# Eight small stores of pieces of x to the output's place in the middle of an attention decode kernel

## The chip, the cores and the metric

The kernel runs on one core of a Trainium2 chip. The metric is the device time of one execution in microseconds (us), lower is better. A time is the median of several runs. A change of the time is called real only beyond 0.2%, 1.37 us here.

## The reference

One decode step of attention with a cache, gated by a GLU block. All tensors are float32; D = 512, 32 heads of 128, 8192 cached positions, F = 1376.

```python
xn = layernorm(x)                                   # x: 1 x 1 x 512
q = (xn @ wq) as 32 heads of 128
p = softmax(q . k_cache * 128 ** -0.5)              # over 8192 positions of each head
s = (p . v_cache) as 1 x 4096 @ wo
g = silu((sigmoid(xn @ w_gate) * (xn @ w_up)) @ w_down)
return x + s * g                                    # 1 x 1 x 512
```

Each of the two caches holds 32 x 8192 x 128 values, 134 MB, and each value is used once.

## The kernel before

**Tiling.** Two heads are treated at a time, so there are NP = 16 pairs. The keys of one pair are 2 x 8192 x 128 values; they lie as 128 partitions of 16384 values (64 KB) in one of two slots, `slots[0]` and `slots[1]`, used in turn. The values of a pair lie the same way in `slots[2]`, of which there is one.

**One pair.** `scores(i)` (line 410) is VectorE's part: it multiplies the keys in place by the query (line 415), sums the products over the 128 elements of each position (line 416), and takes the maximum (line 418). ScalarE makes the exponentials (`powers_of`, line 426). TensorE runs a loop of its own, written down as notes and played at the end (`pair`, line 376, recorded with `Later`; therefore all its instructions stand under line 38): it spreads the maximum, then multiplies the weights with the values and counts `valued` up when it has read the whole of them.

**The order of the transfers.** All large loads are issued by SyncE (SP) on one hardware queue, q1, in the order in which the program is written; what SyncE waits for holds back everything behind it. The queue's transfers are carried by 16 DMA engines. In the loop over pairs (line 440), step i first lets SyncE issue the keys of pair i, once the sums of pair i-2 have freed their slot (line 444, through `load_keys` and `load` at line 168), then the values of pair i-1, once TensorE has read those of pair i-2 (line 446, `load_values`, line 227). So at step i = 8 SyncE issues the keys of pair 8 and the values of pair 7, and the next thing in its program is, at step 9, the wait for the sums of pair 7 and the keys of pair 9.

**The start and the end.** x comes in by ScalarE's queue into `x_row` (line 240): 128 of its values in each of four partitions 32 apart, all the rest of the 128 x 128 tile being zero from a memset (line 239). `x_row` is written nowhere else; it is read by the layer norm at the start and by the last addition (line 541). The GLU block runs at the start too, on the first slots. After the last pair, wo is loaded in eight pieces and multiplied by TensorE and VectorE as they land. SyncE then waits for the last addition and stores the result, four rows of 512 bytes, to the output (line 564), clears the semaphores (line 569), and waits for the store's 16 counts on `s_out` (line 571).

Of the kernel before, what the change touches and what calls it, by code (L numbers as in the profile page):

```python
# [13 lines left out]
P = 128  # L14
# [37 lines left out]
def kernel(  # L52
# [17 lines left out]
    HP = P // 2  # L70
    NB = S // HP
    NP = H // 2
    NG = 4
    GP = P // NG
# [22 lines left out]
    DVE, ACT, SP, POOL = nc.vector, nc.scalar, nc.sync, nc.gpsimd  # L97
# [6 lines left out]
    s_out = nc.alloc_semaphore("s_out")  # L104

    def sb(name, *shape):
        return nc.alloc_sbuf_tensor(name, [P, *shape], F32)[:]
# [11 lines left out]
    x_row, g_row = sb("x_row", GC), sb("g_row", GC)  # L119
# [17 lines left out]
    NK = 8  # L137
# [36 lines left out]
    def wait(eng, *steps):  # L174
        for s in steps:
            if s is not None:
                eng.wait_ge(*s)
# [24 lines left out]
    def rows_of(src, i):  # L202
        rows = src.rearrange("b h s d -> (b h s) d")[2 * i * S:2 * (i + 1) * S, :]
        return rows.rearrange("(p j) d -> p (j d)", p=P)
# [3 lines left out]
    def pieces(*ends):  # L208
        return [slice(a, b) for a, b in zip((0,) + ends, ends + (NB,))]
# [3 lines left out]
    def cols(j):  # L213
        return slice(j.start * Dh, j.stop * Dh)

    def load_keys(i, cut, *after):
        n = (i + 1) % 2
        wait(SP, *after)
        for j in cut:
            ld_k.setdefault(i, []).append((j, load(SP, f"k{n}_{j.start}", slots[n][:, cols(j)], rows_of(k_cache, i)[:, cols(j)])))  # L220

    def load_values(i, cut, *after):

        wait(SP, *after)
        for j in cut:
            sem = s_val[((0,) + V_CUTS).index(j.start)]
            SP.dma_start(slots[2][:, cols(j)], rows_of(v_cache, i)[:, cols(j)]).then_inc(sem, 16)  # L227
# [33 lines left out]
    t = dve(DVE.reduce_sum(st[:, 0:1], x_col, axis=AX.X))  # L261
    wait(PE, t)
    t = pe(PE.matmul(pt[:, 0:1], ones, st[:, 0:1], start=True, stop=True))
    wait(DVE, t)
    t = dve(DVE.tensor_scalar(st[:, 1:2], pt[:, 0:1], 1.0 / D, None, op0=ALU.mult))
    wait(DVE, t)
    t = dve(DVE.tensor_scalar(xc, x_col, st[:, 1:2], None, op0=ALU.subtract))
    wait(DVE, t)
    t = dve(DVE.tensor_mul(sq, xc, xc))
    wait(DVE, t)  # L270
    t = dve(DVE.reduce_sum(st[:, 2:3], sq, axis=AX.X))
    wait(PE, t)
    t = pe(PE.matmul(pm[:, 0:1], ones, st[:, 2:3], start=True, stop=True))
    wait(ACT, t)
    t = act(ACT.activation(st[:, 3:4], pm[:, 0:1], AF.Sqrt, bias=eps_t, scale=1.0 / D))
    wait(DVE, t)
    t = dve(DVE.reciprocal(st[:, 4:5], st[:, 3:4]))
# [8 lines left out]
    def in_place(w, k, cols=slice(None)):  # L286
        y = w[:, 0, cols]
        if k == 0:
            return dve(DVE.tensor_scalar(y, y, xn[:, 0:1], None, op0=ALU.mult))
        return dve(DVE.scalar_tensor_tensor(y, w[:, k, cols], xn[:, k:k + 1], y, op0=ALU.mult, op1=ALU.add))  # L290
# [3 lines left out]
    for k in range(KT - 1):  # L294
        wait(DVE, ld_wq[k // 2] if k % 2 == 0 else None, t if k else None)
        t = in_place(wq_t, k)
# [7 lines left out]
    for t in range(NQ):  # L304
        c = slice(t * QT, (t + 1) * QT)
# [26 lines left out]
    rows = []  # L332
    chunks = [slice(c, min(c + QT, F)) for c in range(0, F, QT)]
    sums = (big[0], po, wide[0]), (big[1], wide[1], wide[2])
    for dst, src, ld in zip(sums, (wg_t, wu_t), (ld_g, ld_u)):
        wait(DVE, ld)
        for k in range(KT):
            t = in_place(src, k)
# [7 lines left out]
    for d, c in zip(sums[0], chunks):  # L346
        t = act(ACT.activation(sg[:, c], d[:, :c.stop - c.start], AF.Sigmoid))
    wait(DVE, t, rows[1])
    for d, c in zip(sums[1], chunks):
        t = dve(DVE.tensor_mul(hg[:, c], sg[:, c], d[:, :c.stop - c.start]))  # L350
# [6 lines left out]
    n = FL // NG  # L357
    for g in range(NG):
        r = slice(g * GP, (g + 1) * GP)
        h = hg[r, NG * FW + g * n:NG * FW + (g + 1) * n].rearrange("p (i c) -> p c i", c=FC)  # L360
        t = dve(DVE.transpose(hid[r, FP:, :].rearrange("p c (i m) -> p c i m", m=NG),
                              h.unsqueeze(3).to_broadcast([GP, FC, n // FC, NG])))
    wait(PE, t, ld_d)
    for c in range(FP + FC):
        g = c % NG * GP
# [40 lines left out]
    def all_max(i):  # L406
        DVE.wait_ge(turned, i + 1)
        DVE.reduce_max(mx[:1, 1:3], pt[0:1, :].rearrange("o (e p) -> o e p", e=2), axis=AX.X).then_inc(reduced, 1)  # L408

    def scores(i):  # L410
        k = slots[(i + 1) % 2].rearrange("p (j d) -> p j d", d=Dh)
        for j, ld in ld_k[i]:
            wait(DVE, ld)
            n = j.stop - j.start
            wait(DVE, dve(DVE.tensor_mul(k[:, j, :], k[:, j, :], qb[:, i:i + 1, :].to_broadcast([P, n, Dh]))))  # L415
            summed[i] = dve(DVE.reduce_sum(sc[i % 2][:, j], k[:, j, :], axis=AX.X))  # L416
        wait(DVE, summed[i])
        DVE.reduce_max(mx[:, 0:1], sc[i % 2], axis=AX.X).then_inc(maxed, 1)

    def heads_out(i):  # L420
        DVE.wait_ge(picked, i + 1)
        o = o_t[:, 2 * WP * i:2 * WP * i + Dh].rearrange("r (e a) -> r a e", a=WP)
        turned_out[i] = dve(DVE.transpose(o, pn.rearrange("e (a r) -> e a r", r=WR)))  # L423


    def powers_of(i):
        ACT.wait_ge(spread_m, i + 1)
        wait(ACT, act(ACT.mul(nb, pm[:, :2], -SCALE)))  # L428
        for e, h in enumerate(HALF):
            ACT.activation(weights[h, :, e * HT:(e + 1) * HT], sc[i % 2][h].rearrange("p (g b) -> p g b", b=HT),  # L430
                           AF.Exp, bias=nb[h, e:e + 1], scale=SCALE, accum_out=rs[h]).then_inc(powers, 1)

    def parts(i):
        ACT.wait_ge(added, i + 1)
        t = act(ACT.copy(den[:GP, 2 * i:2 * i + 2], pm[:GP, 2:]))
        ACT.wait_ge(valued, i + 1)
        ACT.copy(o1, po).then_inc(copied, 1)  # L437
        return t

    for i in range(NP):  # L440
        if i > 0:
            all_max(i - 1)
        if i >= 2:
            load_keys(i, pieces(*K_CUTS.get(i, ())), summed[i - 2])
            if i < NP - 1:
                load_values(i - 1, FULL, (valued, i - 1))
        if i == NP - 1:
            for v, cut in ((i - 1, V_HALVES), (i, V_THREE)):
                load_values(v, cut[:1], (halved, v))
                load_values(v, cut[1:], (valued, v))  # L450
        scores(i)
        if i > 0:
            powers_of(i - 1)
            parts(i - 1)
            heads_out(i - 1)
        if i == 1:
            wait(DVE, c_sig)
            c_gate = dve(DVE.tensor_mul(g_row, g_row, big[1][:, :GC]))
# [48 lines left out]
    for k, r in enumerate(W_DVE):  # L507
        n = k % 2
# [30 lines left out]
    t = dve(DVE.tensor_mul(g_row, g_row, acc))  # L539
    wait(DVE, t)  # L540
    t = dve(DVE.tensor_add(g_row, g_row, x_row))  # L541
# [18 lines left out]
    body.close()  # L560
    nc.switch_bb("leave")

    wait(SP, t)
    SP.dma_start(out.rearrange("a b (g c) -> (a b g) c", g=NG), g_row[0:P:GP, :]).then_inc(s_out, 16)


# [1 line left out]
    assert not unused and used == list(range(used[0], used[0] + len(used)))  # L568
    SP.sem_clear(range(used[0], used[-1] + 1))

    SP.wait_ge(s_out, 16)
    SP.nop().then_inc(s_out, -16)


# [26 lines left out]
```

## Time and profile before

| What | Value |
|---|---|
| Median of 3 runs | 685.09 us (684.86 to 685.15) |
| Profiled execution, its own time | 685.13 us |
| Span of the instructions in it | 683.8 us |
| VectorE (DVE) busy | 613.6 us, 90% of the span |
| TensorE (PE) matmuls busy | 227.5 us, 33% |
| Bytes read from HBM | 293.67 MB, 429 GB/s over the span |
| Packets of the transfers | 7264, of them 824 under 512 B |

In the rows of a profile an engine's name is followed by the line of the kernel, the operation, and the names of the tiles as output<-inputs. A q behind an engine's name (SPq, ACTq) marks its instruction queue, as for an issue of a DMA. In a timeline the two leading numbers are the start and the duration in us; a bracket at the end gives the idle time before the instruction and what ended it. In a list of waits the numbers are us in total, times, and the longest. In a table by stretch each engine has its busy time and its number of instructions; the last three columns are the granted TensorE clock, the share of 16 DMA engines that was busy, and GB/s. A packet counts in a stretch with its whole length where it starts, so a short stretch can show a share over 1.

### The profile page before, as it was taken

Reading aid. Unit: us, or ns where it says so; the run is one execution under the profiler, and the core shown is the slowest. Engines: PE = TensorE matmul, PEld = TensorE weight load, DVE = VectorE, ACT = ScalarE, POOL = GpSimd, SP = SyncE. Lnnn points to the kernel's source line nnn. Section 1 sums busy time; section 2 is a strip of 40 time slices with the busy share of each in tenths; the row PEclk is TensorE's granted clock in tenths of the full one; section 3 lists DMA queues with packets and bytes.
Section 4 is the critical chain, followed back from the end, with each engine's and each line's share of the span. In section 5 each row is a group of like instructions: output and inputs, shape, how many; then the busy total and the mean of one; then the engine's idle time right before and its main releaser. Section 6 shows DMA issues by size and latency. Waiting matters only on the chain. (4 is left out here: it accounts for less than half of the span.)

```text
span 683.8 us, 3412 instructions
## 1 busy us (share of the span) xinstructions
PE 227.5 (33%) x1386; PEld 64.6 (9%) x1386; DVE 613.6 (90%) x151; ACT 44.6 (7%) x142; POOL 2.6 (0%) x11
## 2 busy tenths in 40 slices
PE   0363024050513305060513306060512406050777
PEld 0120001010100101010100101010100101010121
DVE  3869999999999998997989898998989899999926
ACT  2130010000000101000000100000010100000010
POOL 0000000000000000000000000000000000000000
PEclk9986557575665757575665757575665757575699
DMA  9999999999999999999999999999999999999997
GB/s 378 430 442 472 429 429 429 429 429 429 429 429 429 429 429 456 449 445 429 429 429 429 429 429 429 429 429 429 460 456 433 429 414 414 460 418 439 429 411 327
DMA packets 7264, 293.67 MB, mean 429 GB/s; under 512 B 824, under 2 KB 832, under 8 KB 1504
## 3 DMA queue, kind: packets, MB, share of 16 engines
q1 hardware_dynamic: 7256, 293.67, 99.4%
q10 hardware_dynamic: 8, 0.00, 0.0%
HBM read 293.67 MB, written 0.00 MB: 429 GB/s over the span
## 5 line engine op out<-in xcount | busy, mean ns | idle before, releaser
L415 DVE TENSOR_TENSOR slot<-slot,q_all 128x16384 f32<-128x16384 f32 (+3 forms) x18 | 275.7, 15319 | 22.8 <-DMA slot<-in_A_k_cache_dram 22.7
L416 DVE TENSOR_REDUCE sc<-slot 128x128 f32<-128x16384 f32 (+3 forms) x18 | 275.8, 15323 | 0.6
L38 PE MATMUL psum<-slot,zeros 128*8 128x512 f32 x1028 | 153.0, 753 | 249.1 <-PEq L38 249.1
L38 PEld LDWEIGHTS psum<-slot,zeros 128*8 128x8 f32 x1028 | 31.1, 104 | 356.3 <-issue 356.3
L38 PE MATMUL psum<-ident,mx 128*1 128x128 f32 x32 | 8.3, 356 | 115.2 <-PEq L38 115.2
L437 ACT COPY o<-psum 128x512 f32<-128x512 f32 x16 | 9.4, 586 | 398.3 <-PE psum L38 398.3
L38 PE MATMUL psum<-slot,ones 128*128 (+3 forms) x36 | 17.4, 657 | 21.7 <-PEq L38 16.2
L290 DVE SCALAR_TENSOR_TENSOR slot<-slot,xn 128x1376 f32<-128x1376 f32 (+1 forms) x8 | 18.9, 2360 | 3.0 <-DMA slot<-in_A_wq_dram 2.7
L38 PE MATMUL psum<-o,pick 128*2 128x128 f32 x128 | 16.5, 272 | 12.8 <-PEq L38 12.8
L423 DVE STREAM_TRANSPOSE psum<-psum 32x128 f32<-32x128 f32 x16 | 5.0, 310 | 9.5 <-PE psum L38 9.5
L38 PE MATMUL psum<-slot,o_all 128*1 128x128 f32 (+1 forms) x60 | 12.5, 421 | 1.8 <-DMA slot<-in_A_wo_dram 1.7
L38 PEld LDWEIGHTS psum<-ident,mx 128*1 128x1 f32 x32 | 1.8, 80 | 119.4 <-issue 119.4
L428 ACT ACTIVATE nb<-psum 128x2 f32<-128x2 f32 x16 | 2.8, 172 | 157.3 <-PE psum L38 157.3
L430 ACT ACTIVATE zeros<-sc,nb 64x128 f32<-64x128 f32 x32 | 12.8, 399 | 0.9
L38 PEld LDWEIGHTS psum<-o,pick 128*2 128x2 f32 x128 | 9.9, 84 | 29.9 <-issue 27.5
L38 PE MATMUL psum<-zeros,rs 128*32 128x2 f32 x32 | 3.8, 188 | 23.5 <-PEq L38 23.5
L408 DVE TENSOR_REDUCE mx<-psum 1x2 f32<-1x128 f32 x16 | 4.5, 279 | 7.7 <-PE psum L38 7.7
L38 PE MATMUL psum<-mx,ones 1*128 1x2 f32 x32 | 8.5, 333 | 7.4 <-PEq L38 7.4
L38 PE MATMUL psum<-slot,o 128*1 128x512 f32 x26 | 6.3, 1025 | 11.6 <-DMA slot<-in_B_w_down_dram 11.6
L38 PEld LDWEIGHTS psum<-slot,ones 128*128 128x128 f32 (+1 forms) x36 | 6.9, 216 | 32.0 <-issue 24.1
L515 DVE SCALAR_TENSOR_TENSOR q_all<-slot,o_all,q_all 128x512 f32<-128x512 f32 x12 | 8.1, 747 | 2.0 <-DMA slot<-in_A_wo_dram 2.0
L38 PEld LDWEIGHTS psum<-mx,ones 1*128 1x128 f32 x32 | 7.6, 292 | 13.9 <-issue 13.9
(54 smaller groups left out, 62.2 us busy)
## 6 DMA issues: line engine op xcount, KB each, us to landing
slot<-in_A_v_cache_dram SPq DMA_DIRECT2D x3, 4096.0 KB, 23.5
slot<-in_A_wq_dram SPq DMA_DIRECT2D x2, 4096.0 KB, 16.3
slot<-in_A_k_cache_dram SPq DMA_DIRECT2D x2, 4096.0 KB, 37.8
slot<-in_A_k_cache_dram SPq DMA_DIRECT2D x1, 6144.0 KB, 37.9
slot<-in_B_w_gate_dram SPq DMA_DIRECT2D x1, 2752.0 KB, 26.7
slot<-in_B_w_up_dram SPq DMA_DIRECT2D x1, 2752.0 KB, 32.6
slot<-in_B_w_down_dram SPq DMA_DIRECT2D x1, 2560.0 KB, 23.2
slot<-in_A_v_cache_dram SPq DMA_DIRECT2D x1, 2560.0 KB, 9.7
```

Of the source, the lines that this page charges most:

```text
L38: ins = getattr(self.engine, name)(*args, **kwargs)
L290: return dve(DVE.scalar_tensor_tensor(y, w[:, k, cols], xn[:, k:k + 1], y, op0=ALU.mult, op1=ALU.add))
L408: DVE.reduce_max(mx[:1, 1:3], pt[0:1, :].rearrange("o (e p) -> o e p", e=2), axis=AX.X).then_inc(reduced, 1)
L415: wait(DVE, dve(DVE.tensor_mul(k[:, j, :], k[:, j, :], qb[:, i:i + 1, :].to_broadcast([P, n, Dh]))))
L416: summed[i] = dve(DVE.reduce_sum(sc[i % 2][:, j], k[:, j, :], axis=AX.X))
L423: turned_out[i] = dve(DVE.transpose(o, pn.rearrange("e (a r) -> e a r", r=WR)))
L428: wait(ACT, act(ACT.mul(nb, pm[:, :2], -SCALE)))
L430: ACT.activation(weights[h, :, e * HT:(e + 1) * HT], sc[i % 2][h].rearrange("p (g b) -> p g b", b=HT), AF.Exp, bias=nb[h, e:e + 1], scale= ...
L437: ACT.copy(o1, po).then_inc(copied, 1)
L515: ins = DVE.scalar_tensor_tensor(part[n], wo_t[:, r, :], col, part[n], op0=ALU.mult, op1=ALU.add)
```

## The change

At step 8 of the loop, between the issue of the values of pair 7 and that of the keys of pair 9, SyncE issues eight more DMAs. Each reads 64 float32 elements of `x_row` and writes them to one eighth (256 bytes) of the output in HBM. Their shapes, partitions x elements: 4 x 16 from partitions 32 apart (twice), 4 x 16 from neighbouring partitions (twice), 16 x 4 from neighbours, 16 x 4 from partitions 8 apart, 64 x 1, and 1 x 64. Each adds 16 to `s_out` when it is done. Ahead of the result's store SyncE now also waits until `s_out` has reached 128, so that the result is written over what the eight stores left; the last wait and the reset of `s_out` are adapted.

```diff
+    extra = 0
     for i in range(NP):
         if i > 0:
             all_max(i - 1)
...
                 load_values(v, cut[1:], (valued, v))
+        if i == 8:
+            pieces_of = out.rearrange("a b (n c) -> n (a b c)", n=8)
+            for n, src in enumerate((x_row[0:P:GP, :2 * NK], x_row[0:P:GP, :2 * NK], x_row[0:NG, :2 * NK],
+                                     x_row[0:NG, :2 * NK], x_row[0:16, :NG], x_row[0:P:8, :NG], x_row[0:HP, :1],
+                                     x_row[0:1, :HP])):
+                rows = pieces_of[n:n + 1, :].rearrange("o (g c) -> (o g) c", g=src.shape[0])
+                SP.dma_start(rows, src).then_inc(s_out, 16)
+                extra += 16
         scores(i)
...
-    wait(SP, t)
+    wait(SP, t, (s_out, extra))
     SP.dma_start(out.rearrange("a b (g c) -> (a b g) c", g=NG), g_row[0:P:GP, :]).then_inc(s_out, 16)
...
-    SP.wait_ge(s_out, 16)
-    SP.nop().then_inc(s_out, -16)
+    SP.wait_ge(s_out, extra + 16)
+    SP.nop().then_inc(s_out, -extra - 16)
```

## The prediction, made before the result was known

> **What bounds the kernel now.** I read the page first: busy shares, slices, DMA queues, and the chain that ended last.
>
> ```profile
> span 683.8 us, 3412 instructions
> PE 227.5 (33%) x1386; PEld 64.6 (9%) x1386; DVE 613.6 (90%) x151; ACT 44.6 (7%) x142; POOL 2.6 (0%) x11
> ...
> DMA  9999999999999999999999999999999999999997
> ...
> q1 hardware_dynamic: 7256, 293.67, 99.4%
> ...
> DMA 4%; PE 1%; SPq 1%; DVE 0%; issue 0%
> ```
>
> Two things are nearly full: VectorE at 90% and SyncE's one transfer queue (q1) at 99.4% of 16 engines. Which of them sets the pace where the stores go is read from that stage: the timeline of VectorE, and then the stretch between two key multiplies by engine.
>
> ```profile
> 351.48 17.23 DVE L415 TENSOR_TENSOR slot<-slot,q_all 128x16384 f32<-128x16384 f32 x1 [2.83 <-DMA slot<-in_A_k_cache_dram]
> 368.74 17.22 DVE L416 TENSOR_REDUCE sc<-slot 128x128 f32<-128x16384 f32 x1
> 390.08 17.23 DVE L415 TENSOR_TENSOR slot<-slot,q_all 128x16384 f32<-128x16384 f32 x1 [2.75 <-DMA slot<-in_A_k_cache_dram]
> ```
>
> ```profile
> core 0: us, PE busy (x) PEld busy (x) DVE busy (x) ACT busy (x) POOL busy (x), PEclk, DMA share, GB/s
> 351.40:390.00 38.60, 11.07 (x78) 3.23 (x78) 35.24 (x5) 1.89 (x7) 0.00 (x0) 0.63 1.00 435
> 652.00:680.30 28.30, 24.17 (x124) 5.35 (x124) 12.30 (x25) 1.89 (x7) 0.00 (x0) 0.94 0.98 415
> ```
>
> VectorE works 35.24 us of each 38.60 us pair of heads and then stands idle, 2.83 and 2.75 us, for the keys. The transfers have no such idle time: share 1.00 at 435 GB/s, and still 0.98 in the last stage, whose end is the landing of wo. So in the middle the queue is the bound, and the rule for this kernel is simple: **time that the 16 DMA engines lose moves the end by as much; time lost elsewhere costs nothing while the queue has work in it.**
>
> How much work it holds when the stores are issued comes from SyncE's own timeline and its landing times.
>
> ```profile
> 341.52 0.33 SPq L227 DMA_DIRECT2D slot<-in_A_v_cache_dram  x1
> 347.31 0.33 SPq L168 DMA_DIRECT2D slot<-in_A_k_cache_dram  x1
> 379.64 0.33 SPq L227 DMA_DIRECT2D slot<-in_A_v_cache_dram  x1
> ```
>
> ```profile
> slot<-in_A_v_cache_dram SPq DMA_DIRECT2D x2, 29.5
> slot<-in_A_k_cache_dram SPq DMA_DIRECT2D x2, 42.7
> ```
>
> The loop step i=8 issues the keys of pair 8 (before this stretch; they release the multiply at 351.48), then the values of pair 7 at 341.52. Values issued at 341.52 land after about 29.5 us, near 371. The keys of pair 9, issued at 347.31, land after 42.7 us, at 390.0. So a transfer waits behind some 20 us of older ones before it begins.
>
> **The change, part by part.** It removes nothing. It adds eight DMA issues on SyncE between the two upper rows of that timeline, eight small transfers in the ring between the values of pair 7 and the keys of pair 9, and a second semaphore to wait for ahead of the result's store. No other engine's program is touched, and the stores wait for nothing.
>
> *Issue time on SyncE.* The keys of pair 9 stand behind the eight issues, and they wait for the sums of pair 7 anyway:
>
> ```profile
> SPq L168 <- DVE sc L416: 5.5, 1, 5.5
> ```
>
> That is the wait in the stretch from 341.9 to 348 us: SyncE stands there 5.5 us with nothing to do. What one issue costs, from the only small ones in the trace, the result's store of four rows and the load of x by ScalarE's queue, and from the groups of wo loads (shortest/median/longest):
>
> ```profile
> 682.08 0.64 SPq L564 DMA_DIRECT2D out_dram<-g_row  x1
> ...
> 2.38 1.08 ACTq L168 DMA_DIRECT2D x_row<-in_A_x_dram  x1
> ```
>
> ```profile
> L168 SPq DMA_DIRECT2D slot<-in_A_wo_dram x8: 430/444/3821, 648.9 to 652.3; - x8
> ```
>
> Eight at 0.64 us are 5.1 us, which fits into the 5.5 us. Eight at 1.08 us are 8.6 us, and the keys would be issued 3.1 us late. Late issue costs nothing at first: the keys cannot begin before the values are through, near 371 us, and begin about 1.2 us after an issue (the result's store is issued at 682.08 and its packets stand at 683.3, below). So they are in time until about 369.5 us, 22 us after 347.31. Cover for the issue time: the values' own transfer. Cost taken: 0; the price without cover is a rival below. The values of pair 8 come next on SyncE, issued at 379.64, 32 us after the keys, so a delay of some us has gone by then.
>
> *Engine time of the stores.* The trace has one small store to HBM, the result's. Its packets, by the queue's view from 683.0 us and by stretches around it:
>
> ```profile
> DMA packets 8, 0.00 MB, mean 3 GB/s; under 512 B 4, under 2 KB 8, under 8 KB 8
> ```
>
> ```profile
> 682.10:683.30 1.20, 0.00 (x0) 0.00 (x0) 0.00 (x0) 0.00 (x0) 0.00 (x0) 1.00 0.00 0
> 683.30:683.40 0.10, 0.00 (x0) 0.00 (x0) 0.00 (x0) 0.00 (x0) 0.00 (x0) 1.00 0.09 21
> 683.40:683.76 0.36, 0.00 (x0) 0.00 (x0) 0.00 (x0) 0.00 (x0) 0.00 (x0) 1.00 0.00 0
> ```
>
> Four rows give eight packets: four of data and four under 512 B, which I read as one completion for each engine that took part. Their engine time is 0.09 x 16 engines x 0.10 us = 0.144 us, 18 ns for each. Now count the stores, one data packet for each row: 4+4+4+4+16+16+64+1 = 113; completions at one per engine used, 4x4 + 16+16+16 + 1 = 65. Together 178, at 18 ns 3.2 us of engine time. Spread evenly over 16 engines that is 0.20 us. An engine that takes part in every store has 4 + 1 + 1 + 4 + 1 = 11 data packets and 8 completions, 19 x 18 ns = 0.34 us. Lower bound: 0, because the engines do not arrive together. At the seam itself, 369.9 to 372.0 us, the completions of the values and the first packets of the keys are these 32:
>
> ```profile
> DMA  0009999990900000000000000000000000000000
> ...
> DMA packets 32, 1.05 MB, mean 499 GB/s; under 512 B 16, under 2 KB 16, under 8 KB 16
> ```
>
> The slices are 2.1/40 = 0.05 us, and the engines pass the seam over eight of them, 0.4 us. Whoever is early can take small packets without holding up the last. Upper bound, if all 113 and eight completions went through one engine: 121 x 18 ns = 2.2 us. I take 0.2 us, the even spread, nearest to the row with four rows on four engines. A gain is excluded here: nothing is taken out of a queue that never idles.
>
> *The extra wait at the end.* The result's store waited for VectorE alone; now it waits for a second semaphore that has long been reached. One separate wait instruction, by the nearest row, TensorE's:
>
> ```profile
> L38 PEldq EVENT_SEMAPHORE  x7: 51/51/51, 370.8 to 389.3; - x7
> ```
>
> 0.05 us, on the path that ends the run; at most twice that with the step between instructions. I take 0.1 us. Below nothing is excluded.
>
> *Sum.* 0 (issue) + 0.2 (engines) + 0.1 (wait) = +0.3 us. The profiled execution took 685.13 us (683.8 span, 1.3 around it); the median of the runs, 685.09, is 0.04 from it. So **685.4 us**, no change that can be told: 0.2% is 1.37 us, about what a measurement of this kernel can tell from none.
>
> **The rivals.**
>
> *A, the ring waits for each store's receipt* (slower). If a store's completion holds its engine until HBM has confirmed the write, every engine that carries all eight stands eight times. The price of one is at most the stretch after the last packet, 683.40 to the end, 0.36 us: 8 x 0.36 = 2.9 us, 688.3 us. It decides from (1.37 - 0.3)/8 = 0.13 us for each store. With the whole way of the result's store, 682.08 to 683.76, as the price it would be 8 x 1.7 = 13.4 us, 698.8 us. For it: the trace holds no store in front of other work. Against it: at the seam at 370 us completions pass with no gap, inside a stretch of share 1.00; but those go to SBUF. The Trainium skill, "DMA: Bandwidth & Descriptors", section "Anatomy of one DMA — SWDGE (gpsimd) path", says that most of a transfer's fixed 2.0 us is the wait for the target's write receipt, and longest for HBM; eight in a row would by that figure be an estimated 16 us, 701 us, if the ring stood still meanwhile, which no run here shows. Chance 0.09.
>
> *B, every small row pays a round trip.* Rows of 4 to 256 bytes may each be read back and merged before the engine goes on. With 0.36 us as price and 11 data packets on the busiest engine: 4.0 us, 689.4 us. It decides from 1.07/11 = 0.10 us each. Against it: the result's rows, written at 18 ns a packet, but they have 512 bytes. The Trainium skill, same page, section "Specifications", states that below 512 B a DMA engine does a read-modify-write, and its section "Latency and other measured facts" gives an HBM access as 0.2 us on average; 11 of those are an estimated 2.2 us, 687.6 us. The 18 ns row does not speak to it, its data packets being just at that size. Chance 0.05.
>
> *C, the keys are issued too late.* If each store's issue took the longest row, 3.82 us, eight take 30.6 us, from 341.85 to 372.4; the keys follow and begin 1.2 us later at 373.6, while the values are through at 371.0: 2.6 us of empty queue, 688.0 us. It decides from (369.5 - 341.85)/8 = 3.5 us an issue. That longest issue was the eighth wo load, behind seven others and two value pieces, so a full ring seems its reason; here the ring holds the rest of one load, the values and the small stores. Chance 0.02.
>
> *D, one engine takes all the rows.* The 2.2 us above: 687.6 us with the wait. Against it: four rows of the result made four completions. Chance 0.02.
>
> **How the numbers follow.** Forecast (0 to 0.34 us of engine time, 0.05 to 0.1 us of wait, and the spread of the runs, 684.86 to 685.15): 0.79, its own range 684.8 to 685.9. A to D: 0.18, all slower. Left over, something that I do not see and that gains: 0.03. So faster 0.03, same 0.79, slower 0.18. The range reaches up over most of the upper bound of the engine time, 2.0 of its 2.2 us above the median and the wait, for the unknown price of a small write: 684.8 to 687.2 us; A, B and C in full stay outside, 0.16.
>
> **What would show it.** In the changed profile: 178 or so more packets under 512 B in q1, all other sizes unchanged; HBM written 2 KB more; the eight issues on SyncE inside the stretch from 341.85 to about 347; the key multiply that stood at 390.08 at most 0.4 us later against the one at 351.48; share 1.00 there. A or B would show as that multiply coming 1 us or more late with an idle stretch of VectorE longer than 2.8 us, and a DMA share under 0.97 between the two; C as a keys issue after 369 us. The prediction is wrong if the distance of these two multiplies grows by more than 1 us, or if the last stage, from 652 us on, changes its length.

## The result and the profile after

The changed kernel takes **690.29 us** (median of 4 runs, 690.04 to 691.46) against 684.98 us before it on the same chip (684.85 to 685.15): a ratio of **1.0082, 95% interval 1.0069 to 1.0094**. It is slower by 5.3 us, far outside the forecast's range of 684.8 to 687.2 us. The profiled execution took 690.09 us, 4.96 more than that of before; its span is 688.4 us, 4.6 more.

From the page of the changed kernel, the packets and the queue:

```profile
span 688.4 us, 3421 instructions
...
DMA packets 7442, 293.68 MB, mean 427 GB/s; under 512 B 1002, under 2 KB 1010, under 8 KB 1682
...
q1 hardware_dynamic: 7434, 293.67, 99.5%
```

There are 178 more packets under 512 B (1002 - 824), the number that the forecast had counted, and the queue is as full as before. The timeline of VectorE around the seam, and then SyncE's:

```profile
351.64 17.22 DVE L415 TENSOR_TENSOR slot<-slot,q_all 128x16384 f32<-128x16384 f32 x1 [2.84 <-DMA slot<-in_A_k_cache_dram]
395.35 17.23 DVE L415 TENSOR_TENSOR slot<-slot,q_all 128x16384 f32<-128x16384 f32 x1 [7.87 <-DMA slot<-in_A_k_cache_dram]
434.03 17.23 DVE L415 TENSOR_TENSOR slot<-slot,q_all 128x16384 f32<-128x16384 f32 x1 [2.83 <-DMA slot<-in_A_k_cache_dram]
```

```profile
341.81 0.33 SPq L227 DMA_DIRECT2D slot<-in_A_v_cache_dram  x1
342.18 4.13 SPq L458 DMA_DIRECT2D out_dram<-x_row  x8
347.46 0.38 SPq L168 DMA_DIRECT2D slot<-in_A_k_cache_dram  x1
```

The multiply of step 8 starts where it did (351.64, before 351.48), that of step 9 comes 43.71 us later instead of 38.60, and the one after that is back at 38.68. The whole loss, **5.1 us, lies in this one step**: VectorE waits 7.87 us for the keys of pair 9 instead of 2.75. SyncE is not the reason: the eight issues take 4.13 us, and the keys are issued at 347.46 (before 347.31). What happened to the transfers shows in two stretches after the stores, and in the whole step:

```profile
core 0: us, PE busy (x) PEld busy (x) DVE busy (x) ACT busy (x) POOL busy (x), PEclk, DMA share, GB/s
351.60:395.30 43.70, 11.20 (x78) 3.27 (x78) 35.24 (x5) 1.89 (x7) 0.00 (x0) 0.62 1.00 384
372.60:380.40 7.80, 7.26 (x60) 1.54 (x52) 7.80 (x1) 0.47 (x1) 0.00 (x0) 0.87 0.99 252
380.40:390.00 9.60, 2.41 (x14) 1.41 (x14) 6.51 (x4) 1.42 (x7) 0.00 (x0) 0.73 0.99 430
```

The engines count as busy throughout (share 0.99 to 1.00), but from 372.6 to 380.4 us they move 252 GB/s, and afterwards 430 again. The loss doesn't show as idle time; it shows only in the last column. The trace also records every packet with its length, and there the loss can be seen. The 178 packets of the stores themselves are short, 9 to 18 ns each, 1.6 us in all or 0.10 us for each engine. But 27 of the 64 KB packets of keys behind them, begun between 370.3 and 377.5 us, last up to 7.5 us, where every such packet of the kernel before lasts 2.42 us in this stretch. What they last beyond 2.42 us adds up to 4.9 us for each of the 16 engines, nearly the whole loss.

What the end shows: the result's store is issued 0.32 us after the start of the last addition in both kernels (682.08 - 681.76 before; here the two rows are at 686.78 and 686.46), so the second semaphore costs nothing. The last addition is 4.70 us later, and not 5.27 as the multiply of step 9 (395.35 - 390.08), because the last stage ran a little shorter. Over the runs below that stage and the rest differ by up to about 1 us either way; therefore **the distance of the two multiplies is taken as the measure of the loss**, and the time of the runs beside it.

### The profile page after: what moved, and what is told of

Read it like the earlier page. It is cut to its first block, busy times and chain, and to the rows that moved or that the text cites. A ratio compares the mean times of both kernels' runs of the same rounds, so it can differ in the third digit from the quotient of the medians.

```text
span 688.4 us, 3421 instructions
## 1 busy us (share of the span) xinstructions
PE 225.0 (33%) x1386; PEld 64.2 (9%) x1386; DVE 613.7 (89%) x151; ACT 44.6 (6%) x142; POOL 2.6 (0%) x11
## 2 busy tenths in 40 slices
DMA packets 7442, 293.68 MB, mean 427 GB/s; under 512 B 1002, under 2 KB 1010, under 8 KB 1682
## 5 line engine op out<-in xcount | busy, mean ns | idle before, releaser
L38 PE MATMUL psum<-slot,zeros 128*8 128x512 f32 x1028 | 150.1, 743 | 254.2 <-PEq L38 254.2
```

The source lines that it names most:

```text
L38: ins = getattr(self.engine, name)(*args, **kwargs)
```

## The experiments

Each kernel is the changed kernel with other stores in the same place of SyncE's program (run 12: of ScalarE's), and so has a wait for their completions at the end. None computes less of the result. "Loss" is the distance of the key multiplies of steps 8 and 9 less the 38.60 us of before, in the one execution that was profiled. In the four runs that lose 0.1 us or less it is 38.61 to 38.68 us.

**1. The column store alone (e1_col64)**

```diff
-            for n, src in enumerate((x_row[0:P:GP, :2 * NK], ..., x_row[0:HP, :1], x_row[0:1, :HP])):
+            for n, src in enumerate((x_row[0:HP, :1],)):
```

> Only the store of 64 rows of 4 bytes stays, 64 of the change's 113 data packets, one of its eight stores; what it loses is read as the distance of the key multiplies of steps 8 and 9, 38.60 us before and 43.71 with all eight, 5.1 us more. Theory 'each packet': every data packet to HBM holds a shared path for 5.1/113 = 0.045 us, so 64 x 0.045 = 2.9 us, distance 41.5. Theory 'each store': every store's receipt costs 5.1/8 = 0.64 us, distance 39.2. Theory 'once': the turn from reading to writing costs 5.1 us however little is written, distance 43.7.

Measured: 690.72 us, ratio 1.0096 (1.0076 to 1.0115). VectorE's timeline:

```profile
351.81 17.23 DVE L415 TENSOR_TENSOR slot<-slot,q_all 128x16384 f32<-128x16384 f32 x1 [2.84 <-DMA slot<-in_A_k_cache_dram]
396.02 17.22 DVE L415 TENSOR_TENSOR slot<-slot,q_all 128x16384 f32<-128x16384 f32 x1 [8.57 <-DMA slot<-in_A_k_cache_dram]
```

Distance 44.21, loss 5.6 us. This one store, 64 rows of 4 bytes written to 256 contiguous bytes, loses as much as all eight together.

**2. The other seven stores (e2_no_col64)**

```diff
-                                     x_row[0:NG, :2 * NK], x_row[0:16, :NG], x_row[0:P:8, :NG], x_row[0:HP, :1],
-                                     x_row[0:1, :HP])):
+                                     x_row[0:NG, :2 * NK], x_row[0:16, :NG], x_row[0:P:8, :NG], x_row[0:1, :HP])):
```

> The other seven stores, without the 64 rows of 4 bytes: 49 data packets. Each packet: 49 x 0.045 = 2.2 us, distance of the two key multiplies 40.8 us. Each store: 7 x 0.64 = 4.5 us, 43.1. Once: 43.7. A fourth, 'the packets of 4 bytes alone are the matter', has 38.6 here and all 5.1 us in the run with the 64 rows.

Measured: 685.35 us, ratio 1.0008 (0.9998 to 1.0017), which cannot be told from no change.

```profile
352.03 17.23 DVE L415 TENSOR_TENSOR slot<-slot,q_all 128x16384 f32<-128x16384 f32 x1 [3.02 <-DMA slot<-in_A_k_cache_dram]
391.01 17.23 DVE L415 TENSOR_TENSOR slot<-slot,q_all 128x16384 f32<-128x16384 f32 x1 [3.13 <-DMA slot<-in_A_k_cache_dram]
```

Loss 0.38 us. "Each store" (4.5 us) and "once" (5.1 us) fall, and "each packet" alike (2.2 us) as well. Seven of the eight stores cost what the forecast had put for all.

**3. The same eight to SBUF (e4_to_sbuf)**

```diff
-                rows = pieces_of[n:n + 1, :].rearrange("o (g c) -> (o g) c", g=src.shape[0])
-                SP.dma_start(rows, src).then_inc(s_out, 16)
+                SP.dma_start(sink[0:src.shape[0], at:at + src.shape[1]], src).then_inc(s_out, 16)
+                at += src.shape[1]
```

> The same eight reads of x, in the same shapes and in the same place of the queue, but to a spare tile in SBUF instead of the output in HBM, so the small rows and the completions stay and the writes to HBM go. If writing to HBM is the cause (each packet, each store or once alike): distance 38.6 to 38.8 us and a time within 0.1% of before. If small packets, odd shapes or completions cost wherever they go: 43.7 us, and 690 us.

Measured: 685.67 us, ratio 1.0011 (1.0001 to 1.0021).

```profile
351.59 17.23 DVE L416 TENSOR_TENSOR slot<-slot,q_all 128x16384 f32<-128x16384 f32 x1 [2.83 <-DMA slot<-in_A_k_cache_dram]
390.73 17.23 DVE L416 TENSOR_TENSOR slot<-slot,q_all 128x16384 f32<-128x16384 f32 x1 [3.30 <-DMA slot<-in_A_k_cache_dram]
```

Loss 0.54 us, a little above the 0.2 us expected: small packets to SBUF are nearly free, the column's 64 among them. (The row of 64 elements went as 16 pieces here, so q1 had 30 packets more than in the changed kernel, 7464 against 7434.) So neither the reads of x nor the number of small packets and completions makes the large loss. That it needs HBM as the target is not shown, for in SBUF the column's rows land in 64 partitions, and not side by side as in the output.

**4. Eight stores of 4 x 16 (e6_rows64)**

```diff
-            for n, src in enumerate((x_row[0:P:GP, :2 * NK], ...)):
+            for n, src in enumerate([x_row[0:P:GP, :2 * NK]] * 8):
```

> Eight stores of the first shape, 4 rows of 64 bytes each, one to each eighth of the output: 32 data packets, eight stores, on four engines only. Each packet: 32 x 0.045 = 1.4 us, distance 40.0 us. Each store: 5.1 us, 43.7. Once: 43.7. If only packets of a few bytes are slow: near 38.6.

Measured: 685.52 us, ratio 1.0007 (0.9998 to 1.0017); distance 38.97, loss 0.37 us. Packets of 64 bytes, one after the other over the 2 KB of the output, cost next to nothing. What is left in runs 2, 3 and 4, 0.4 to 0.5 us, goes with seven or eight transfers, whatever their target; it was not taken apart further.

So the question became what is special in the column store: the size of its packets, their number, or where they go.

**5. The column's packets far apart (f1_far)**

```diff
+    scratch = nc.dram_tensor("scratch", (HP, 4352), F32, kind="Internal").ap()
...
+            SP.dma_start(scratch[:, :1], x_row[0:HP, :1], allow_slow_non_contiguous=True).then_inc(s_out, 16)
```

> The store of 64 rows of 4 bytes alone, as before, but to a scratch tensor in HBM with 17,408 bytes from one row to the next, so that no two packets write near each other. Theory 'same spot': the 64 packets of the column store all write one stretch of 256 bytes and wait for one another there; then the loss goes, distance of the key multiplies 38.6 to 39.0 us instead of 44.2. Theory 'each small packet': a packet of 4 bytes costs about 5.6/64 = 0.088 us of a shared path wherever it goes; then 44.2 again.

Measured: 684.76 us, ratio 0.9995 (0.9985 to 1.0004).

```profile
351.66 17.23 DVE L417 TENSOR_TENSOR slot<-slot,q_all 128x16384 f32<-128x16384 f32 x1 [3.04 <-DMA slot<-in_A_k_cache_dram]
390.28 17.22 DVE L417 TENSOR_TENSOR slot<-slot,q_all 128x16384 f32<-128x16384 f32 x1 [2.77 <-DMA slot<-in_A_k_cache_dram]
```

Loss 0.02 us. The same 64 packets of 4 bytes, as many completions and the same read of x, and nothing is lost. So **neither the number nor the size of the packets is the cause by itself; what differs is where they land.** Two things differ there: the rows are far apart, and they go to a scratch tensor in HBM instead of the output. No run writes the contiguous column to a scratch tensor, so this run against run 1 cannot tell the two apart; run 10 against run 13 below, both to a scratch tensor, can, for a smaller loss. The first 64 KB packets of keys, all 16 of them begun between 370.15 and 370.85 us, in this run and in run 1:

```profile
370.15:370.85 0.70, 0.00 (x0) 0.00 (x0) 0.70 (x1) 0.00 (x0) 0.00 (x0) 0.50 3.53 1499
```

```profile
370.15:370.85 0.70, 0.00 (x0) 0.00 (x0) 0.70 (x1) 0.00 (x0) 0.00 (x0) 0.50 6.89 1499
```

The bytes are the same, and a packet counts with its whole length where it starts: 3.53 x 16 x 0.70 us make 39.5 us of packets, 6.89 make 77.2, some 2.4 and 4.8 us for each of the 16. The small packets are recorded with 9 ns each in both runs. The stretch behind the stores in this run and in the changed kernel, both 10 us from 370.4:

```profile
370.40:380.40 10.00, 9.32 (x64) 1.92 (x64) 10.00 (x1) 0.00 (x0) 0.00 (x0) 0.72 1.04 452
```

```profile
370.40:380.40 10.00, 8.79 (x64) 1.86 (x64) 10.00 (x1) 0.47 (x1) 0.00 (x0) 0.79 1.00 236
```

452 GB/s with the packets far apart, 236 in the changed kernel, where the column's lie together, at the same busy share.

**6 to 8. Other numbers and sizes, close together (f2_rows64x16B, f3_rows16x4B, f4_rows128x4B)**

```diff
+            flat = out.rearrange("a b (n c) -> n (a b c)", n=1)
+            SP.dma_start(flat[:, :256].rearrange("o (g c) -> (o g) c", g=64), x_row[0:64, :4]).then_inc(s_out, 16)
```

and likewise with 16 and with 128 rows of one element.

> One store of 64 rows of 16 bytes, the first 1,024 bytes of the output: as many packets as the column store, the same engines, four times the bytes of each, four packets instead of 16 in each 64 bytes. Same spot, by the number of packets that share 64 bytes: a quarter, 1.4 us, distance 40.0. Each packet under 512 B whatever its size: 5.6 us, 44.2. Each packet of 4 bytes only: 38.6 to 39.0.

> One store of 16 rows of 4 bytes, one for each engine, the first 64 bytes of the output. Each small packet, one after the other: 16 x 0.088 = 1.4 us, distance 40.0 us. Same spot with separate stretches of 64 bytes side by side (the column store has four of them): all 5.6 us, 44.2, as one stretch has its 16 packets here too. Once: 44.2.

> One store of 128 rows of 4 bytes, 512 bytes of the output, twice the column store. Each small packet: 128 x 0.088 = 11.3 us, distance 49.9 us. Same spot with separate stretches of 64 bytes: 5.6 us, 44.2. Once: 44.2.

Measured: 64 rows of 16 bytes 686.19 us, ratio 1.0020 (1.0010 to 1.0030), distance 39.47, loss 0.87. 16 rows of 4 bytes 685.79 us, 1.0010 (1.0001 to 1.0020), 39.07, loss 0.47. 128 rows of 4 bytes 693.95 us, 1.0123 (1.0106 to 1.0140), loss 8.6:

```profile
352.16 17.23 DVE L415 TENSOR_TENSOR slot<-slot,q_all 128x16384 f32<-128x16384 f32 x1 [2.84 <-DMA slot<-in_A_k_cache_dram]
399.33 17.23 DVE L415 TENSOR_TENSOR slot<-slot,q_all 128x16384 f32<-128x16384 f32 x1 [10.48 <-DMA slot<-in_A_k_cache_dram]
```

No expectation fits all three. The loss grows with the number of packets, but not in proportion (16, 64, 128 rows: 0.5, 5.6, 8.6 us), and it does not stay the same either, as it would if each 64 bytes with its 16 packets were worked off beside the next.

**9 to 11. The same 64 packets, dealt out otherwise (g1_across, g2_within, g3_pitch64)**

```diff
+            SP.dma_start(flat[:, :HP].rearrange("o (j e) -> (o e) j", e=16), x_row[0:16, :NG], allow_slow_non_contiguous=True).then_inc(s_out, 16)
```

```diff
+    scratch = nc.dram_tensor("scratch", (16, 16), F32, kind="Internal").ap()
...
+            SP.dma_start(scratch[:, 0:8:2], x_row[0:16, :NG], allow_slow_non_contiguous=True).then_inc(s_out, 16)
```

```diff
+    scratch = nc.dram_tensor("scratch", (HP, 16), F32, kind="Internal").ap()
...
+            SP.dma_start(scratch[:, :1], x_row[0:HP, :1], allow_slow_non_contiguous=True).then_inc(s_out, 16)
```

> 64 packets of 4 bytes into the same 256 bytes of the output, but dealt out otherwise: the four packets of one engine go 64 bytes apart, and each stretch of 64 bytes gets one packet from each of 16 engines (in the column store it gets four each from four engines). Theory 'shared stretch', whoever writes: as the column store, distance of the key multiplies 44.2 us. Theory 'own engine', an engine waits where its own packets follow each other into one stretch: 39.1 or less.

> 64 packets of 4 bytes to a scratch tensor: the four of one engine lie 8 bytes apart in one stretch of 64 bytes, and each engine has a stretch of its own, 16 stretches in 1,024 bytes. Shared stretch: four packets share instead of 16, like the rows of 16 bytes (which lost 0.9 us): 39.0 to 39.5. Own engine: 44.2. If what is shared is wider than 64 bytes (256 bytes hold 16 of these packets, as in the rows of 16 bytes): 39.5; if it is 1,024 bytes or more: 44.2.

> The column's 64 rows of 4 bytes to a scratch tensor with 64 bytes from one row to the next, 4,096 bytes in all; with 17,408 bytes between rows the loss was gone (38.62 us). Shared stretch of 64 bytes or fewer: gone again, 38.6. A wider shared stretch, 256 bytes (four packets each): 38.7 to 39.5; the whole 4,096 bytes: 44.2.

Measured: across the engines 691.84 us, ratio 1.0099 (1.0082 to 1.0116), loss 6.3:

```profile
352.00 17.23 DVE L415 TENSOR_TENSOR slot<-slot,q_all 128x16384 f32<-128x16384 f32 x1 [2.83 <-DMA slot<-in_A_k_cache_dram]
396.85 17.22 DVE L415 TENSOR_TENSOR slot<-slot,q_all 128x16384 f32<-128x16384 f32 x1 [9.00 <-DMA slot<-in_A_k_cache_dram]
```

Within one engine's own 64 bytes 685.76 us, 1.0009 (0.9999 to 1.0019), distance 39.73, loss 1.1. One packet every 64 bytes 684.79 us, 0.9996 (0.9987 to 1.0006), distance 38.61, loss 0.01. "Own engine" falls: it does not help that an engine's own packets go to different places, as long as all lie in the same 256 bytes. (Which engine carries which row is inferred from the order of the rows; the traces do not name it.) And at 64 bytes apart the loss is already gone.

**12. The column store from ScalarE's queue (g4_act)**

```diff
-                SP.dma_start(rows, src).then_inc(s_out, 16)
+            ACT.dma_start(pieces_of[6:7, :].rearrange("o (g c) -> (o g) c", g=HP), x_row[0:HP, :1]).then_inc(s_out, 16)
```

> The column store alone, unchanged but issued by ScalarE on its own hardware queue in the same loop step instead of by SyncE. If what is held up is SyncE's ring, in which the keys stand behind the stores: the loss goes, the sum of the distances of the key multiplies from step 7 to step 9 stays at 77.3 us (before 38.68 + 38.60) and the time within 0.2% of before. If it is a path that the engines share, reads of other rings included: the sum is 77.3 + 5.6 = 82.9 us, wherever in the two steps it falls.

Measured: 691.76 us, ratio 1.0094 (1.0077 to 1.0110). The key multiplies of steps 7, 8 and 9:

```profile
312.93 17.23 DVE L415 TENSOR_TENSOR slot<-slot,q_all 128x16384 f32<-128x16384 f32 x1 [2.74 <-DMA slot<-in_A_k_cache_dram]
357.76 17.23 DVE L415 TENSOR_TENSOR slot<-slot,q_all 128x16384 f32<-128x16384 f32 x1 [8.98 <-DMA slot<-in_A_k_cache_dram]
397.14 17.22 DVE L415 TENSOR_TENSOR slot<-slot,q_all 128x16384 f32<-128x16384 f32 x1 [3.73 <-DMA slot<-in_A_k_cache_dram]
```

The two distances sum to 84.21 us, 6.9 above the 77.28 of before. The store no longer stands in the loads' ring; it begins earlier (the loss falls on step 8), and holds up the loads of the other ring by even more than the 5.6 us of run 1. So it is no matter of the order in one ring: the large transfers are slowed by something that they share with the small writes. Whether that is the DMA engines themselves or lies behind them, no run separates.

**13 to 15. How near is near (h1_apart, h2_pitch32, h3_rows32x4B)**

```diff
+    scratch = nc.dram_tensor("scratch", (16, 256), F32, kind="Internal").ap()
...
+            SP.dma_start(scratch[:, 0:8:2], x_row[0:16, :NG], allow_slow_non_contiguous=True).then_inc(s_out, 16)
```

The second is run 11 with rows of 8 elements in place of 16, the third run 6 with 32 rows of one element.

> As the 64 packets of 4 bytes of which each engine writes its four, 8 bytes apart, into one stretch of 64 bytes (1.1 us lost, 39.73 us), but the 16 stretches now lie 1,024 bytes apart, so that 256 bytes hold four packets instead of 16. Four packets share 64 bytes as before. Theory 'a stretch of 64 bytes or fewer is what is shared': 39.7 again. Theory '256 bytes or more': nothing lost, as with one packet every 64 bytes, where 256 bytes held four too (38.61).

> The column's 64 rows with 32 bytes from one to the next: two share each 64 bytes. If the shared stretch is 32 bytes: 38.6 us. If it is 64 bytes: between nothing and the 1.1 us of four packets for each stretch, 38.8 to 39.3.

> One store of 32 rows of 4 bytes, contiguous, two packets for each of 16 engines: between the 16 rows (0.5 us) and the 64 (5.6). If each packet beyond the first few costs the same, 5.1/48 = 0.107 us for each of the 16 more: 0.5 + 1.7 = 2.2 us, distance 40.8. If one stretch of 64 bytes works beside the next: 0.5 us, 39.1, as each stretch has 16 packets in all three.

Measured: four packets in each 64 bytes, these stretches 1,024 bytes apart, 684.70 us, 0.9998 (0.9989 to 1.0008), loss 0.1:

```profile
351.62 17.23 DVE L417 TENSOR_TENSOR slot<-slot,q_all 128x16384 f32<-128x16384 f32 x1 [2.79 <-DMA slot<-in_A_k_cache_dram]
390.29 17.23 DVE L417 TENSOR_TENSOR slot<-slot,q_all 128x16384 f32<-128x16384 f32 x1 [2.83 <-DMA slot<-in_A_k_cache_dram]
```

One every 32 bytes 684.92 us, 1.0005 (0.9996 to 1.0015), distance 38.61, loss 0.01. 32 rows of 4 bytes, contiguous, 689.43 us, 1.0068 (1.0047 to 1.0089), loss 3.5:

```profile
351.73 17.23 DVE L415 TENSOR_TENSOR slot<-slot,q_all 128x16384 f32<-128x16384 f32 x1 [2.85 <-DMA slot<-in_A_k_cache_dram]
393.79 17.23 DVE L415 TENSOR_TENSOR slot<-slot,q_all 128x16384 f32<-128x16384 f32 x1 [6.21 <-DMA slot<-in_A_k_cache_dram]
```

Four packets in 64 bytes are thus harmless by themselves (h1) and cost 1.1 us when the next 64 bytes hold four more and so on (g2): the stretch that counts is wider than 64 bytes. Of what was written down before, the line for 32 bytes fits run 14 by itself, but runs 10 and 13 both have four packets in 32 bytes, one with the loss and one without; run 11 lies just under the 38.7 us put for 256 bytes, and run 15 fits neither of its lines (2.2 and 0.5 us). So no rule found here gives the size of the loss. All the runs that make one store, in order of how many packets fall into each 256 bytes:

| Store | Packets | in 64 bytes | in 256 bytes | Loss, us |
|---|---|---|---|---|
| rows 17,408 bytes apart (f1) | 64 x 4 B | 1 | 1 | 0.0 |
| one each 64 bytes (g3) | 64 x 4 B | 1 | 4 | 0.0 |
| four in 64 bytes, 1,024 apart (h1) | 64 x 4 B | 4 | 4 | 0.1 |
| one each 32 bytes (h2) | 64 x 4 B | 2 | 8 | 0.0 |
| 16 rows, contiguous (f3) | 16 x 4 B | 16 | 16 | 0.5 |
| rows of 16 bytes, contiguous (f2) | 64 x 16 B | 4 | 16 | 0.9 |
| four in each 64 bytes (g2) | 64 x 4 B | 4 | 16 | 1.1 |
| 32 rows, contiguous (h3) | 32 x 4 B | 16 | 32 | 3.5 |
| 64 rows, contiguous (e1) | 64 x 4 B | 16 | 64 | 5.6 |
| the same, dealt out otherwise (g1) | 64 x 4 B | 16 | 64 | 6.3 |
| 128 rows, contiguous (f4) | 128 x 4 B | 16 | 64 | 8.6 |

With up to 8 packets in 256 bytes nothing is lost, with 16 up to about 1 us, beyond that several. Each of these losses is that of one execution. The medians of the runs less those of before have the same three groups (none above 0 with up to 8 packets, 0.6 to 1.2 us with 16, 4.5 to 9.0 beyond), but within a group they do not rank the runs: f2, with packets of 16 bytes, has 1.2 us and g2, with 4 bytes, 0.6, and the executions of h3 alone took 688.28 to 691.10 us. So at equal density no effect of a packet's size is clear of this spread.

The clean pair is g2 and h1: the same 64 packets, both to a scratch tensor, and only the distance of the stretches differs. The losses above 1.1 us are all of stores to the output; no run tells whether a scratch tensor would lose as much.

That 256 bytes are the width is not shown; the column only puts the runs in the right order. Counted by 512 bytes, f2 and h3 would be alike with 32 packets each, and they lost 0.9 and 3.5 us; 128 bytes would order the runs about as well as 256. Nor is it shown what holds up the loads: the records show their packets lasting longer, and not why.

## Why the prediction was wrong, point by point

- **What bounds the kernel** held. The queue's lost time went to the end one for one: the 5.1 us of the seam came out as 4.96 in the profiled execution and 5.3 in the median, and the step after it is back at 38.68 us.
- **Issue time** held: 4.13 us for eight (forecast 5.1), the keys issued 0.15 us later than before, and nothing waits for it. Rival C is out.
- **The count of packets** held to the packet, 178. So does that of the completions, one for each engine that took part; rival D is out.
- **The step that failed is "engine time of the stores": what a data packet costs the queue.** I priced a packet by the 18 ns for which it keeps an engine, and let the keys behind it run at their full rate; what the stores do to the loads behind them was thus put at nothing, without a row for it. The part that was priced is of the right size: 0.10 us for each engine was recorded where 0.20 was taken, and the seven stores without the column lost 0.38. The part put at nothing is the loss: behind the column store the 64 KB packets of keys last up to 7.9 us instead of 2.42, and this store alone lost 5.6 us. The row of the result's store could not show it: its four packets go to four places 512 bytes apart and nothing runs behind them, while the column store puts 64 into 256 bytes with the keys behind it. The upper bound of 2.2 us was no bound for the same reason: it counted only the time of the small packets.
- **The extra wait** cost nothing, 0.1 was put.
- **Rivals A and B** had the right side and the wrong mechanism. A (a receipt for each store) would show in seven stores as 7 x 0.36 = 2.5 us; 0.38 was measured. B (each small row pays a round trip) would show with the 64 rows far apart, which lost 0.02. B came nearest in its size, 4.0 us, but a row costs something only near its neighbours, and then not as time of its own packet (9 ns) but of the loads behind it. The Trainium skill, "DMA: Bandwidth & Descriptors", section "Specifications", names a read-modify-write below 512 B, which the prediction put beside B; 64 packets of 4 bytes at no cost (f1) mean that, whatever is done inside, being under 512 B is not by itself what costs here.
- **What would show it** was half right. The late multiply and VectorE's longer wait (7.87 us) came, but the share of the DMA engines, which I expected under 0.97, stayed at 1.00. A 64 KB packet that lasts 7.5 us counts as busy all the while; the rate, 384 GB/s against 435, tells it.

The chances put 0.14 on a write that is dearer than it looks. That was little for a kind of transfer, small writes to HBM in front of other work, of which the trace of before had no example; and the range ended at 2.0 us because I let that bound of packets times time stand for ignorance of the price.

## What to carry to other kernels

A small store is to be judged by where its rows land, not by its bytes: 64 rows of 4 bytes to one 256-byte stretch of the output delayed the loads of the core by 5.6 us, the same 64 rows 32 bytes or more apart in a scratch tensor by nothing, and 256 bytes written as rows of 64 or 256 bytes by next to nothing. So where loads fill the queue, it can pay to gather a column across partitions into a few rows before it is stored, or to store its rows apart; what the gathering costs was not measured. Issuing the store from another queue did not help. And when transfers seem full, compare the rate, not the busy share, before and after.

## What was unexpected of the hardware

- The packets of 4 bytes do not look slow themselves: 9 ns each in every run, while the 64 KB packets behind the column store last up to 7.9 us.
- A held-up transfer reads as busy: share 1.00 at 236 GB/s and 1.04 at 452 in the same 10 us of two runs.
- Few bytes can hold up the loads, from their own ring or from the other: the column store has 256 bytes, and issued from ScalarE's queue it cost the loads on SyncE's 6.9 us.
- The loss is not in proportion to the rows: 16, 32, 64 and 128 contiguous rows of 4 bytes lost 0.5, 3.5, 5.6 and 8.6 us. The executions with 32 rows differ by 2.8 us among themselves, and why the step from 16 to 32 is so steep stays open.
- The same rows to SBUF, with all eight stores, lost 0.5 us; there the column's rows land in 64 partitions.
